# The output weights' product with the gate columns, with the gate columns standing in four column tiles and a summing product behind it

## The chip, the cores and the metric

The kernel runs on one core of a Trainium2 chip. The metric is the device time of one execution in microseconds; the time before is 626.16 us, the median of three runs (625.21 to 626.29).

## What is computed

Sliding-window attention (4 batches, 8 heads, 576 rows, 64 columns a head) is followed by a gated feed-forward layer and a mixture of experts whose choice can be held from row to row. The change lies in the second of the three, where the feed-forward layer's output meets the gate of the third:

```python
h = np.maximum(x @ w_in, 0.0)
# three taps along the rows, then
gate = 1.0 / (1.0 + np.exp(-conv_out))
y = (h * gate @ w_out)                       # (2304, 512)
logits = np.einsum('bsd,de->bse', y, w_gate) # 8 experts
local  = np.einsum('bsd,de->bse', y, w_local) # one more column
...
out[b, s] = p[e] * (np.maximum(y[b, s] @ w1[e], 0.0) @ w2[e])
```

The kernel doesn't form the logits from `y`: it multiplies `w_out` by the nine gate columns once, and appends the ten columns that result (one of them zero) to `w_out`, so that one matmul gives `y` and the logits.

## The kernel before

Rows of the sequence are handled a batch at a time. `ffn(b)` runs over eight blocks of 128 hidden columns (KF = 8) and, for each, two halves of 288 rows: twelve matmuls a half (L470; weights and `x` are held as a high and a low part in fp32r, and three products are summed), then ReLU (L477), three taps and the gate on ACT and DVE (L489 to L493), and a split of the gated block into `gH` and `gL` (L498, L499). `ffn_out(i)` (L512) multiplies 128 rows of the gated block with `woutH` and `woutL`, in two column halves; the second half (260 wide) holds the ten gate columns. `attention(b + 1)` runs beside `ffn(b)`: transposes (L201, L214), scores (L247), softmax (L259 to L284), transposes of the weights (L297, L299) and the product with `v` (L324), whose result is split into `x` by L334 on ACT and L337 on DVE.

The change lies in `conv_out(kk)`, which is called once for each of the eight 128-row blocks of `w_out`, all within `ffn(0)`. The weights come as 64-bit floats: `bits64` (L597, L599, L601, all on DVE) makes a 32-bit block `lf`, and `finish` makes of it

- `woutH` and `woutL` (L629 on ACT, L630 on DVE),
- `psWT`, four transposes on PE (L648), copied by ACT to `wt` (L649),
- `psW`, `wt` times the gate columns `wgl`, four fp32 matmuls that add up in one PSUM bank with `wt` standing and ten columns moving (L652),
- the appended columns of `woutH` and `woutL` (L654 on ACT, L655 on DVE).

`wgl` is filled at the start by two DMAs that POOL issues (L676, L677) behind that of the taps (L675, into `cr`), and its last column is zeroed by DVE (L672). `ident` and `mask` are made on POOL ahead of that.

In this part of the program the order on each engine is set when the kernel is built, by a scheduler that plays the instructions through with the lengths that it assumes; each engine then runs its list in that order. `psWT`, `psW` and the tiles of attention take turns in the four PSUM banks of the pool `psa`; `wt` and the output tiles `ysb` take turns in the two buffers of the pool `y`. The first 54 us or so and the last part (the experts) are written in an order of their own.

Of the kernel before, what the change touches and what calls it, by code (L numbers as in the profile page):

```python
# [8 lines left out]
F32 = mybir.dt.float32  # L9
# [4 lines left out]
AF = mybir.ActivationFunctionType  # L14
# [7 lines left out]
def kernel(  # L22
# [14 lines left out]
    nc = tc.nc  # L37
    w_in, conv_w, w_out = (a.bitcast(U32) for a in (w_in, conv_w, w_out))
    P = 128
    B, H, S, D = q.shape  # L40
    DM = H * D
    FF = w1.shape[2]
    KD = DM // P
    KF = FF // P
    E = w1.shape[0]
# [13 lines left out]
    const = ctx.enter_context(tc.tile_pool(name="const", bufs=1))  # L59
# [8 lines left out]
    ident = const.tile([P, P], F32, name="ident")  # L68
# [5 lines left out]
        nc.gpsimd.affine_select(out=m, in_=m, pattern=[[1, P]], compare_op=ALU.is_ge, fill=NEG, base=-1, channel_multiplier=-1)  # L74
        nc.gpsimd.affine_select(out=m, in_=m, pattern=[[-1, P]], compare_op=ALU.is_ge, fill=NEG, base=64, channel_multiplier=1)
    cw = const.tile([P, 3, KF], F32, name="cw")
    wgl = const.tile([P, KD, E + 2], F32, name="wgl")
    L_all = const.tile([P, NT, E + 2], F32, name="L_all")


    E1 = E + 2
# [4 lines left out]
    psa = p1l.enter_context(tc.tile_pool(name="psa", bufs=4, space=PSUM))  # L86
# [12 lines left out]
    if True:  # L99
# [21 lines left out]
        def bank(b):  # L121

            cyc[0] += 1
            i = cyc[0] % 8
            if b == 0 and i % 4 == 1:
                return psm.tile([P, 512], F32, tag="m", name="psM")
            if b == 0 and i % 4 == 3:
                return pso.tile([P, 512], F32, tag="o", name="psO")
            return psa.tile([P, 512], F32, tag="a", name="psA")
# [47 lines left out]
        def warm(ps, n):  # L177

            w = ident.bitcast(BF16)
            for _ in range(n):  # L180
                nc.tensor.matmul(ps[:, 0:256], w[:, 0:P], w[:, 0:256], start=True, stop=True)
# [411 lines left out]
        def bits64(r, f, steps=range(3)):  # L593

            hi, lo, fb = r[:, :, 1], r[:, :, 0], f.bitcast(U32)
            if 0 in steps:
                nc.vector.tensor_scalar(fb, hi, 3, 0x3FFFFFF8, op0=ALU.logical_shift_left, op1=ALU.bitwise_and)  # L597
            if 1 in steps:
                nc.vector.scalar_tensor_tensor(fb, hi, 0xC0000000, fb, op0=ALU.bitwise_and, op1=ALU.bitwise_or)  # L599
            if 2 in steps:  # L600
                nc.vector.scalar_tensor_tensor(fb, lo, 29, fb, op0=ALU.logical_shift_right, op1=ALU.bitwise_or)  # L601
# [3 lines left out]
        def chunk_in(c, kk):  # L605
            src = w_in.rearrange("(k p) f -> p k f", p=P)
            return src[:, kk, 2 * c * CC:2 * (c + 1) * CC]

        def load_chunk(r, src, eng=nc.sync):
            eng.dma_start(out=r.rearrange("p f t -> p (f t)"), in_=src)  # L610
            return r
# [3 lines left out]
        def quarters(t):  # L615

            return t.rearrange("p (a k i) -> p k a i", k=KD, i=QB)
# [4 lines left out]
        def conv_chunk(src, wH, wL, eng, r=None, view=lambda t: t):  # L622
            if r is None:
                r = load_chunk(cv.tile([P, CC, 2], U32, name="raw", bufs=2), src)
            f = cv.tile([P, CC], F32, name="lf")
            bits64(r, f)

            def finish():
                nc.scalar.activation(wH, view(f), AF.Copy)  # L629
                eng.tensor_tensor(wL, view(f), wH.bitcast(F32), op=ALU.subtract)  # L630

            return f, finish
# [5 lines left out]
        def conv_out(kk):  # L638

            src = w_out.rearrange("(k p) f -> p k f", p=P)  # L640
            f, fin = conv_chunk(src[:, kk, :], quarters(woutH[:, kk, 0:DM]), quarters(woutL[:, kk, 0:DM]), nc.vector, view=by_tile)

            def finish():
                fin()
                wt = y_p.tile([P, KD, P], F32, tag="ysb", name="wt")
                pt = psa.tile([P, 512], F32, tag="a", name="psWT")
                for j in range(KD):
                    nc.tensor.transpose(pt[:, j * P:(j + 1) * P], f[:, j * P:(j + 1) * P], ident)  # L648
                nc.scalar.activation(wt.rearrange("p j f -> p (j f)"), pt, AF.Copy)  # L649
                ps = psa.tile([P, 512], F32, tag="a", name="psW")  # L650
                for j in range(KD):
                    nc.tensor.matmul(ps[:, 0:E1], wt[:, j, :], wgl[:, j, :], start=j == 0, stop=j == KD - 1)  # L652
                wH, wL = woutH[:, kk, DM:DW], woutL[:, kk, DM:DW]
                nc.scalar.activation(wH, ps[:, 0:E1], AF.Copy)  # L654
                nc.vector.tensor_tensor(wL, ps[:, 0:E1], wH.bitcast(F32), op=ALU.subtract)  # L655

            return finish
# [11 lines left out]
        with tc.manual_schedule():  # L669
            warm(bank(0), 6)  # L670
            load_pair(0, 0)
            nc.vector.memset(wgl[:, :, E + 1:E1], 0.0)  # L672
            KC = 3 * KF
            taps = cv.tile([P, CC, 2], U32, tag="raw", name="cr", bufs=2)[0:KC, 0:P]
            nc.gpsimd.dma_start(out=taps.rearrange("r p t -> r (p t)"), in_=conv_w.rearrange("k (f x) -> (k f) x", f=KF))  # L675
            nc.gpsimd.dma_start(out=wgl[:, :, 0:E], in_=w_gate.rearrange("(k p) e -> p k e", p=P))  # L676
            nc.gpsimd.dma_start(out=wgl[:, :, E:E + 1], in_=w_local.rearrange("(k p) e -> p k e", p=P))  # L677
            cin = [(c, kk) for c in range(FF // CC) for kk in range(KD)]
            load_pair(0, 1)

            def stage_chunk(i, eng=nc.sync):
                c, kk = divmod(i, KD)
                early[c, kk] = load_chunk(st_p.tile([P, CC, 2], U32, name=f"raw{i}"), chunk_in(c, kk), eng)

            for i in range(2):
                stage_chunk(i, nc.scalar)
            for i in range(2, KD):
                load_pair(0, i)
                stage_chunk(i)
            part = {}  # L690

            def others(s_, i, g):

                c, kk = divmod(i, KD)
                fs = slice(c * CC, (c + 1) * CC)
                if s_ == "c":
                    if g == 0:
                        part[i] = cv.tile([P, CC], F32, name="lf")
                    bits64(early[c, kk], part[i], (g,))
                elif s_ == "h":  # L700
                    cin.pop(0)
                    nc.scalar.activation(winH[:, kk, fs], part[i], AF.Copy)
                elif s_ == "u":
                    nc.gpsimd.tensor_tensor(winL[:, kk, fs], part[i], winH[:, kk, fs].bitcast(F32), op=ALU.subtract)
                elif s_ == "w":
                    part["f"] = cv.tile([P, CC], F32, tag="lf", name="cf")[0:KC, 0:P]
                    bits64(taps, part["f"])
                elif s_ == "W":
                    part["ps"] = bank(0)
                    nc.tensor.transpose(part["ps"][:, 0:KC], part["f"], ident[0:KC, 0:KC])  # L710
                elif s_ == "Y":
                    nc.vector.tensor_copy(cw.rearrange("p k f -> p (k f)"), part["ps"][:, 0:KC])
                elif s_ == "D":
                    warm(bank(0), i)
                else:
                    nc.gpsimd.memset(qbds[i], 0.0)
                    load_pair(1, i)
                    if i == 0:
                        stage_chunk(4)
                        stage_chunk(5)  # L720

            attention_first(FIRST, others)
# [3 lines left out]
        y_p = p1l.enter_context(tc.tile_pool(name="y", bufs=2))  # L726
# [853 lines left out]
```

## Time and profile before

| | |
|---|---|
| median of three runs | 626.16 us |
| the profiled execution | 626.18 us |
| its span, first to last instruction | 624.5 us |
| mean granted clock of PE | 0.982 |
| PE busy | 593.2 us, 95% |
| DVE busy | 431.0 us, 69% |
| ACT busy | 386.9 us, 62% |
| POOL busy | 221.7 us, 36% |

A share of the whole span is an average over stages that have different limits. The stretch in which the eight blocks of `w_out` are prepared, 59 to 119 us, is a tenth of the span and is best read by itself. Matmuls overlap in the records, and their ends are modelled: the time from one start to the next says more than the length of one. An fp32 matmul stands in the trace as two weight loads and two matmuls, and in an order listing as one row.

### The profile page before, as it was taken

The page shows a single profiled execution, that of the slowest core. Times are in us where ns is not written, and L with a number is a line of the kernel's source. Part 1 is how long each engine was busy: PE and PEld are TensorE (multiplying, and loading weights), DVE is VectorE, ACT ScalarE, POOL GpSimd, SP SyncE. Part 2 cuts the span into 40 slices and gives each one's busy share as a digit, 9 for nine tenths or more (in the row PEclk, how much of TensorE's full clock was granted, in tenths as well). Part 3 has the DMA queues.
Part 4 walks back from the last instruction along what each step waited for, and adds up shares of the span by engine and source line. Part 5 has one row for each costly group of instructions (what it writes and reads, how often), then busy time and mean ns, then how long its engine had stood idle before and what let it go on. Part 6 is the DMA issues. An engine that isn't in the chain of part 4 may idle for free.

```text
span 624.5 us, 12744 instructions
## 1 busy us (share of the span) xinstructions
PE 593.2 (95%) x4503; PEld 533.9 (85%) x4503; DVE 431.0 (69%) x986; ACT 386.9 (62%) x910; POOL 221.7 (36%) x251
## 2 busy tenths in 40 slices
PE   6779999999999999999999989999999999999996
PEld 4658998899999999989987879979899799897774
DVE  4888999645786167852786977658766686576863
ACT  3567778535876357853661556566765676667863
POOL 3412000001223012342250257458567385643740
PEclk9789999799999999999999999999999999999999
DMA  8794515653245201129102289768668763524850
GB/s 188 187 233 120 165 59 114 111 130 82 53 83 100 70 35 37 35 64 273 46 2 34 93 242 358 265 223 292 218 219 307 247 222 123 179 69 144 295 174 16
DMA packets 122614, 92.17 MB, mean 148 GB/s; under 512 B 96594, under 2 KB 97170, under 8 KB 122544
## 3 DMA queue, kind: packets, MB, share of 16 engines
q1 hardware_dynamic: 116064, 79.61, 44.4%
q0 software_dynamic: 4992, 10.24, 4.9%
q10 hardware_dynamic: 1488, 1.44, 0.8%
q8 instruction: 37, 0.61, 0.4%
q14 instruction: 33, 0.27, 0.1%
HBM read 89.53 MB, written 10.71 MB: 161 GB/s over the span
## 4 chain that ended last, share of the span: by engine, by line
PE 61%; DVE 13%; ACT 9%; DMA 9%; issue 5%; SPq 2%; POOL 0%; POOLq 0%; DVEq 0%; ACTq 0%
PE psM L470 14%; PE psO L512 13%; PE psH L1327 8%; PE psO L1362 8%; PE psA L247 3%; PE psO L1341 3%; ACT x L1168 3%; DMA raw<-in_moe_w_dram 3%; PE psA L324 2%; DMA pcur<-p_dram,gidx 2%; PE psA L299 2%; DMA qk<-in_q_dram 2%; DMA raw<-in_moe_w_out_dram 1%; ACT woutH L1168 1%; PE psG L582 1%
## 5 line engine op out<-in xcount | busy, mean ns | idle before, releaser
L499 POOL TENSOR_TENSOR gL<-h,gH 128x64 fp32r<-128x64 f32 (+5 forms) x46 | 43.6, 956 | 216.0 <-ACT gH L498 209.2
L470 PE MATMUL psM<-x,winH 128*128 128x288 f32 x512 | 108.4, 303 | 0.1
L470 PEld LDWEIGHTS psM<-x,winH 128*128 128x128 f32 x512 | 82.0, 189 | 2.4 <-ACT x L334 0.4
L470 PE MATMUL psM<-x,winL 128*128 128x288 f32 x256 | 76.0, 297 | 0.0
L512 PE MATMUL psO<-woutH,gH 128*128 128x262 f32 (+2 forms) x240 | 64.4, 314 | 1.2 <-ACT gH L498 1.0
L512 PE MATMUL psO<-woutL,gH 128*128 128x262 f32 (+2 forms) x240 | 62.2, 305 | 0.0
L512 PE MATMUL psO<-woutH,gL 128*128 128x262 f32 (+2 forms) x240 | 61.2, 304 | 0.0
L1253 POOL DMA_INDIRECT out_dram<-o,sidx x24 | 31.6, 1319 | 79.6 <-ACT o L1295 41.6
L271 ACT ACTIVATE sS<-sS,mx 128x128 f32<-128x128 f32 (+1 forms) x144 | 55.1, 386 | 6.9 <-DVE mx L259 6.8
L1172 DVE TENSOR_TENSOR woutL<-raw,woutH 128x1024 fp32r<-128x1024 f32 x28 | 33.8, 1224 | 29.1 <-ACT woutH L1168 29.1
L1172 DVE TENSOR_TENSOR x<-raw,x 128x1024 fp32r<-128x1024 f32 x42 | 49.9, 1222 | 4.0 <-ACT x L1168 3.8
L1362 PE MATMUL psO<-gH,x 128*128 128x288 f32 x240 | 51.3, 296 | 0.0
L1327 PE MATMUL psH<-gH,woutH 128*128 128x288 f32 x160 | 48.3, 302 | 0.4 <-DVE gL L1330 0.4
L470 PEld LDWEIGHTS psM<-x,winL 128*128 128x128 f32 x256 | 48.4, 189 | 0.1
L1327 PE MATMUL psH<-gL,woutH 128*128 128x288 f32 x160 | 47.4, 296 | 0.0
L1327 PE MATMUL psH<-gH,woutL 128*128 128x288 f32 x160 | 47.3, 295 | 0.0
L512 PEld LDWEIGHTS psO<-woutH,gH 128*128 128x128 f32 x240 | 41.0, 190 | 4.1 <-ACT gH L498 1.6
L1168 ACT ACTIVATE x<-raw 128x1024 fp32r<-128x1024 f32 x42 | 43.0, 1056 | 0.0
L512 PEld LDWEIGHTS psO<-woutL,gH 128*128 128x128 f32 x240 | 41.4, 191 | 1.4
L512 PEld LDWEIGHTS psO<-woutH,gL 128*128 128x128 f32 x240 | 40.9, 191 | 1.2
L259 DVE CUSTOM_DVE_ANT_0 sS<-psA,mask 128x128 f32<-128x128 f32 (+1 forms) x126 | 28.8, 277 | 17.9 <-PE psA L247 15.1
L1362 PEld LDWEIGHTS psO<-gH,x 128*128 128x128 f32 x240 | 39.8, 189 | 0.0
(395 smaller groups left out, 1645.5 us busy)
## 6 DMA issues: line engine op xcount, KB each, us to landing
raw<-in_moe_w_dram SPq DMA_DIRECT2D x104, 512.0 KB
v<-in_v_dram SPq DMA_DIRECT2D x56, 128.0 KB
y_dram<-ysb SPq DMA_DIRECT2D x17, 256.0 KB
raw<-in_moe_w_out_dram SPq DMA_DIRECT2D x8, 512.0 KB
raw<-in_moe_w_dram SPq DMA_DIRECT2D x32, 128.0 KB
raw<-in_moe_w_in_dram SPq DMA_DIRECT2D x6, 512.0 KB
qk<-in_k_dram SPq DMA_DIRECT2D x32, 72.0 KB
qk<-in_q_dram SPq DMA_DIRECT2D x32, 72.0 KB
```

The source lines that it names most:

```text
L247: nc.tensor.matmul(ps[:, j * P + lo:(j + 1) * P], qbd[:, c, :], kT[:, k0:W * (c + 1)], start=True, stop=True)
L259: nc.vector.tensor_tensor_reduce(sS[:, c, lo:P], ps[:, j * P + lo:(j + 1) * P], mask[:, lo:P], -scale, -NEG, op0=ALU.add, op1=ALU.min, acc ...
L271: nc.scalar.activation(sS[:, c, lo:P], sS[:, c, lo:P], AF.Exp, scale=-1.0, bias=mx[:, c:c + 1], accum_out=sume[:, c:c + 1],)
L470: nc.tensor.matmul(ps[:, 0:HS], wt[:, kk, f * P:(f + 1) * P], xt[:, c0:c0 + HS], start=n == 0, stop=n == 3 * KD - 1,)
L499: e1.tensor_tensor(gL[:, f, r:r + m], t[:, done:done + m], gH[:, f, r:r + m].bitcast(F32), op=ALU.subtract)
L512: nc.tensor.matmul(p_[:, 0:cs.stop - cs.start], gt[:, kk, r:r + P], wt[:, kk, cs], start=n == 0, stop=n == 3 * KF - 1,)
L1168: nc.scalar.activation(dst[kk][0], raws[kk], AF.Copy)
L1172: nc.vector.tensor_tensor(L_, raws[kk], H_.bitcast(F32), op=ALU.subtract)
L1253: nc.gpsimd.indirect_dma_start(out=out[:, :], out_offset=bass.IndirectOffsetOnAxis(ap=sidx[0:n, c:c + 1].bitcast(U32), axis=0), in_=o[0:n] ...
L1327: nc.tensor.matmul(ps, a, w, start=n == 0, stop=n == 3 * KD - 1)
L1341: nc.tensor.matmul(ps, a[:, f], w, start=n == 0, stop=n == 3 * KF - 1)
L1362: nc.tensor.matmul(ps, a, w[:, f], start=n == 0, stop=n == 3 * KF - 1)
```

## The change

`wgl` has 32 columns for each of the four blocks of 128 model columns instead of ten; DVE zeroes the 23 behind the gate columns. The four matmuls of `finish` now have `wgl` standing and `wt` moving: each gives 32 rows of 128 columns, in its own quarter of the PSUM partitions (four column tiles), and they don't add up in PSUM. ACT copies the 128x128 result to a new tile `w4`, and a fifth matmul, `psV`, has `w4` standing and a selector `sel` moving, which adds the four quarters and gives the ten columns with the 128 rows on the partitions, as before. `sel` is four pieces of `ident` under one another, made by four POOL copies at the start. `w4` is taken from the pool `y` and `psV` from the pool `psa`.

```diff
-    wgl = const.tile([P, KD, E + 2], F32, name="wgl")
+    wgl = const.tile([P, KD, 32], F32, name="wgl")
+    sel = const.tile([P, E + 2], F32, name="sel")
+    for i in range(0, P, 32):
+        nc.gpsimd.tensor_copy(sel[i:i + 32], ident[i:i + 32, i:i + E + 2])
...
                 for j in range(KD):
-                    nc.tensor.matmul(ps[:, 0:E1], wt[:, j, :], wgl[:, j, :], start=j == 0, stop=j == KD - 1)
+                    nc.tensor.matmul(ps[32 * j:32 * j + 32, 0:P], wgl[:, j, :], wt[:, j, :], start=True, stop=True)
+                w4 = y_p.tile([P, DM], F32, tag="ysb", name="w4")
+                nc.scalar.activation(w4[:, 0:P], ps[:, 0:P], AF.Copy)
+                ps = psa.tile([P, 512], F32, tag="a", name="psV")
+                nc.tensor.matmul(ps[:, 0:E1], w4[:, 0:P], sel, start=True, stop=True)
...
-            nc.vector.memset(wgl[:, :, E + 1:E1], 0.0)
+            nc.vector.memset(wgl[:, :, E + 1:32], 0.0)
```

The scheduler gives the instructions of `ffn(0)` and `attention(1)` another order on PE, ACT and DVE; behind that part the orders are alike but for a few loads. Line numbers of the changed kernel are 3 higher up to the product and 7 higher behind it. Three places at the end of that part follow.

PE before, the last two blocks of `w_out` (`psWT` are the transposes, `psW` the product):

```order
L648 MATMUL psWT<-ident,lf 128x128 [waits DVE_49]
L648 MATMUL psWT<-ident,lf 128x128 x3
L512 MATMUL psO<-woutH,gH 128x262 [waits Activation_49]
L470 MATMUL psM<-x,winH 128x288 [waits Activation_49] x2
L652 MATMUL psW<-wgl,wt 128x10 [waits Activation_49]
L652 MATMUL psW<-wgl,wt 128x10 x3
L512 MATMUL psO<-woutL,gH 128x262 [waits DVE_49]
L512 MATMUL psO<-woutH,gL 128x262
L512 MATMUL psO<-woutH,gH 128x260 [waits Activation_49]
L648 MATMUL psWT<-ident,lf 128x128 [waits DVE_49]
L648 MATMUL psWT<-ident,lf 128x128 x3
L512 MATMUL psO<-woutH,gH 128x262 [waits Activation_49]
```

PE now, from the last `psW` but one on (`psV` is the summing product, `w_` a copy `w4`):

```order
L473 MATMUL psM<-x,winH 128x288 [waits Activation_49]
L473 MATMUL psM<-x,winH 128x288 [waits DVE_49]
L473 MATMUL psM<-x,winL 128x288
L473 MATMUL psM<-x,winH 128x288 [waits DVE_49]
L473 MATMUL psM<-x,winL 128x288
L655 MATMUL psW<-wt,wgl 32x128 [waits Activation_49]
L655 MATMUL psW<-wt,wgl 32x128 x3
L659 MATMUL psV<-sel,w_1558 128x10 [waits Activation_49]
L651 MATMUL psWT<-ident,lf 128x128 [waits DVE_49,PE_49]
L651 MATMUL psWT<-ident,lf 128x128 x3
L515 MATMUL psO<-woutH,gH 128x260 [waits Activation_49]
L515 MATMUL psO<-woutL,gH 128x260 [waits DVE_49]
```

Ahead of the second last `psW` there now stand four matmuls of `ffn(1)`, two of which want DVE's split of `x`; and `psV` stands right behind `psW`. The last row here is followed by the last `psW` and its `psV`.

ACT before, at the same place (`qbd` and `x` belong to attention):

```order
L225 ACTIVATE qbd_127<-psA 64x8x64 [waits PE_49]
L225 ACTIVATE qbd_127<-psA 64x8x64
L498 ACTIVATE gH<-h 128x576 [waits DVE_49]
L629 ACTIVATE woutH<-lf 128x4x4x32 [waits DVE_49]
L334 ACTIVATE x<-psA 128x320 [waits PE_49]
L334 ACTIVATE x<-psA 128x256 [waits PE_49]
L649 ACTIVATE wt<-psWT 128x512 [waits PE_49,Activation_49]
L654 ACTIVATE woutH<-psW 128x10 [waits PE_49]
L629 ACTIVATE woutH<-lf 128x4x4x32 [waits DVE_49]
L649 ACTIVATE wt<-psWT 128x512 [waits PE_49,Activation_49]
L654 ACTIVATE woutH<-psW 128x10 [waits PE_49]
```

ACT now:

```order
L632 ACTIVATE woutH<-lf 128x4x4x32 [waits DVE_49]
L228 ACTIVATE qbd_132<-psA 64x8x64 [waits PE_49]
L228 ACTIVATE qbd_132<-psA 64x8x64
L337 ACTIVATE x<-psA 128x320 [waits PE_49]
L337 ACTIVATE x<-psA 128x256 [waits PE_49]
L652 ACTIVATE wt<-psWT 128x512 [waits PE_49,Activation_49]
L657 ACTIVATE w_1558<-psW 128x128 [waits PE_49,Activation_49]
L661 ACTIVATE woutH<-psV 128x10 [waits PE_49]
L652 ACTIVATE wt<-psWT 128x512 [waits PE_49,Activation_49]
L657 ACTIVATE w_1578<-psW 128x128 [waits PE_49,Activation_49]
L524 ACTIVATE ysb<-psO 128x262 [waits Activation_49]
L661 ACTIVATE woutH<-psV 128x10 [waits PE_49]
```

The last L629 (L632 now) has moved ahead of `qbd`, `x` and the second last `wt`, and the copies `w_` stand between `wt` and the appended columns.

DVE before, from the last block's bits (L601) on:

```order
L601 SCALAR_TENSOR_TENSOR lf<-raw,lf 128x512 [waits DVE_49]
L282 TENSOR_SCALAR sS<-sS,sume 128x64 [waits DVE_49]
L284 TENSOR_TENSOR sS<-sS,sume 128x1024
L337 TENSOR_TENSOR x<-psA,x 128x320 [waits Activation_49]
L337 TENSOR_TENSOR x<-psA,x 128x256 [waits Activation_49]
L655 TENSOR_TENSOR woutL<-psW,woutH 128x10 [waits Activation_49]
L630 TENSOR_TENSOR woutL<-lf,woutH 128x4x4x32 [waits Activation_49]
L655 TENSOR_TENSOR woutL<-psW,woutH 128x10 [waits Activation_49]
```

DVE now:

```order
L604 SCALAR_TENSOR_TENSOR lf<-raw,lf 128x512 [waits DVE_49]
L285 TENSOR_SCALAR sS<-sS,sume 128x64 [waits DVE_49]
L287 TENSOR_TENSOR sS<-sS,sume 128x1024
L221 COPY kT_134<-psA 128x512 [waits PE_49]
L633 TENSOR_TENSOR woutL<-lf,woutH 128x4x4x32 [waits Activation_49]
L340 TENSOR_TENSOR x<-psA,x 128x320 [waits Activation_49]
L340 TENSOR_TENSOR x<-psA,x 128x256 [waits Activation_49]
L207 COPY kT_134<-psA 128x64 [waits PE_49]
L211 COPY qbd_132<-psA 64x64
L212 COPY qbd_132<-psA 64x64
L662 TENSOR_TENSOR woutL<-psV,woutH 128x10 [waits Activation_49] x2
```

The last L601 (L604 now) has the `kT` and `qbd` copies behind it that stood ahead of it. In the whole list up to the last L655 DVE has the same operations as before; ACT has the eight copies more and one output copy (L521) that stood later; and by its last product PE has run eight matmuls more, two each of L470 with `winH` and with `winL`, and two each of L512 with `woutL` and with `gL`.

## Rows read from the trace of the kernel before

**Rows 1.** The page, part 1: busy us, share of the span and instructions of each engine

```profile
PE 593.2 (95%) x4503; PEld 533.9 (85%) x4503; DVE 431.0 (69%) x986; ACT 386.9 (62%) x910; POOL 221.7 (36%) x251
```

**Rows 2.** Busy time by stretches of 10 us, 59 to 119 us: last stretch and sum

```profile
core 0: us, PE busy (x) PEld busy (x) DVE busy (x) ACT busy (x) POOL busy (x), PEclk, DMA share, GB/s
...
109.00:119.00 10.00, 9.11 (x88) 7.79 (x88) 9.36 (x23) 5.60 (x14) 0.00 (x0) 0.94 0.71 128
sum 60.00, PE 56.51 PEld 52.87 DVE 58.51 ACT 46.06 POOL 0.00; mean PE 9.42 PEld 8.81 DVE 9.75 ACT 7.68 POOL 0.00
```

**Rows 3.** The same view, one stretch behind the stage

```profile
135.00:175.00 40.00, 40.00 (x362) 38.63 (x362) 25.36 (x83) 26.39 (x92) 5.61 (x8) 1.00 0.39 81
```

**Rows 4.** Groups by line, 60 to 119 us: busy us, mean ns, idle before, releasers

```profile
L652 PE MATMUL psW<-wgl,wt 128*128 128x10 f32 x64 | 8.4, 260 | 2.0 <-ACT wt L649 1.9
L652 PEld LDWEIGHTS psW<-wgl,wt 128*128 128x128 f32 x64 | 8.1, 197 | 3.0 <-ACT wt L649 3.0
```

**Rows 5.** Timeline of the PE weight loads: start us, us, engine, line, tiles

```profile
64.59 0.99 PEld L652 LDWEIGHTS psW<-wgl,wt 128*128 128x128 f32 x8
65.50 0.75 PEld L247 LDWEIGHTS psA<-kT,qbd 128*128 128x128 f32 x6
66.17 0.47 PEld L214 LDWEIGHTS psA<-ident,qk 128*128 128x128 f32 x4
...
92.99 0.66 PEld L324 LDWEIGHTS psA<-aT,v 128*64 128x64 f32 x20 [0.17 <-issue]
93.72 0.19 PEld L470 LDWEIGHTS psM<-x,winL 128*128 128x128 f32 x1
```

**Rows 6.** Timeline of the end of the stage: ACT, DVE, PE, PE weight loads

```profile
110.56 1.20 ACT L225 ACTIVATE qbd<-psA 64x512 f32<-64x512 f32 x2 [0.74 <-PE psA L214]
...
113.01 0.71 ACT L334 ACTIVATE x<-psA 128x320 fp32r<-128x320 f32 x2
...
115.36 0.18 ACT L654 ACTIVATE woutH<-psW 128x10 fp32r<-128x10 f32 x1 [1.15 <-PE psW L652]
115.53 0.63 ACT L629 ACTIVATE woutH<-lf 128x512 fp32r<-128x512 f32 x1
116.52 0.60 ACT L649 ACTIVATE wt<-psWT 128x512 f32<-128x512 f32 x1 [0.35 <-PE psWT L648]
...
113.60 0.21 DVE L204 COPY kT<-psA 128x64 f32<-128x64 f32 x1
...
114.82 0.68 DVE L601 SCALAR_TENSOR_TENSOR lf<-raw,lf 128x512 uint32<-128x512 uint32 x1
115.42 0.25 DVE L282 TENSOR_SCALAR sS<-sS,sume 128x64 f32<-128x64 f32 x1
115.58 1.22 DVE L284 TENSOR_TENSOR sS<-sS,sume 128x1024 f32<-128x1024 f32 x1
116.83 0.82 DVE L337 TENSOR_TENSOR x<-psA,x 128x320 fp32r<-128x320 f32 x2
...
117.64 0.68 DVE L630 TENSOR_TENSOR woutL<-lf,woutH 128x512 fp32r<-128x512 f32 x1
...
114.27 1.06 PE L652 MATMUL psW<-wgl,wt 128*128 128x10 f32 x8
...
117.17 1.32 PE L652 MATMUL psW<-wgl,wt 128*128 128x10 f32 x8 [0.56 <-ACT wt L649]
...
118.27 1.40 PEld L247 LDWEIGHTS psA<-kT,qbd 128*128 128x128 f32 x6
```

**Rows 7.** Busy time by stretches: the stretch at the lower granted clock

```profile
118.00:124.00 6.00, 6.00 (x29) 5.93 (x29) 1.87 (x14) 2.60 (x13) 0.00 (x0) 0.50 0.63 96
```

**Rows 8.** Timeline of the start: POOL issues the taps, DVE uses them

```profile
2.95 0.75 POOL L675 DMA_DIRECT2D cr<-in_moe_conv_w_dram  x1
...
11.04 0.20 DVE L597 TENSOR_SCALAR cf<-cr 24x128 uint32<-24x128 uint32 x1
...
13.40 0.69 DVE L218 COPY kT<-psA 128x512 f32<-128x512 f32 x1 [0.45 <-PE psA L214]
```

## The prediction

> **What bounds the kernel now.** I read the page's shares first. PE is busy 95% of the span and DVE 69% [rows 1], so one would price the change by what it takes off PE. The change touches only the eight finishes of `conv_out`, though, and they all lie between 59 and 119 us; so I next read the busy time by stretches of that stage. There DVE is busy 58.5 of 60 us, and the PE's 56.5 holds modelled ends and waits [rows 2]. The reader is to see that this stage ends when DVE is through its list: DVE also takes apart the 64-bit weights (L597 to L601), and PE fills in with what is ready. Behind the stage it is the reverse: from 135 to 175 us PE is busy 40.00 of 40 us and DVE 25 [rows 3], and much the same beyond. So whatever delays the moment at which PE is free of the last product is passed on to the end, and what PE does ahead of that moment is taken off again. The groups by line show the product itself: 64 passes on PE, eight for each finish, with 2.0 and 3.0 us of waiting for the ACT copy `wt` before them, in 4 and 5 places [rows 4].
>
> **The product on PE.** Each fp32 matmul is two passes of weight load and matmul. Eight passes with 128 columns standing and 10 moving take from 64.59 to 65.50 us, 0.91 [rows 5], and 8 x 0.91 = 7.3 us in all. Now 32 columns stand and 128 move. No row has four column tiles. From above: L247 has 128 standing and 128 moving, six passes from 65.50 to 66.17, 0.11 each, which is 0.89 for eight: nothing saved. From below: L324 runs 64-column tiles in two halves, 20 passes of 64 moving columns from 92.99 to 93.72, 0.037 each [rows 5]; doubled for 128 columns that is 0.58 for eight, and half of it with four tiles instead of two, 0.29. I take 0.45, between the two readings of L324, the nearest row. The sum behind it is one matmul of the old kind, two passes, 0.91/4 = 0.23. Ahead of L324 the load queue stood 0.17 us for nothing but issue [rows 5]; I charge it once a product. So 0.45 + 0.23 + 0.17 = 0.85 for 0.91: PE saves 8 x 0.06 = 0.5 us, with bounds from 0.29 + 0.23 (3.1 us saved) to 0.89 + 0.23 + 0.17 (3.0 lost).
>
> What L324 shows is that two column halves do overlap, and that entering them costs about 0.17 us. The Trainium skill (TensorEngine Tiling (Array Packing), Performance Considerations) recommends this very swap of standing and moving operand with column tiling, with up to four times the throughput where the free side is 32 or less; its Key Properties say that a change of tiling mode drains TensorE. By the first rule alone the product would cost 0.91/4 = 0.23 and PE would save 3.6 us, an estimate from that page; the second speaks against it, and the 0.17 us agrees with it.
>
> **ACT and the new hop.** Each finish gains a copy of 128x128 out of PSUM. ACT takes 0.18 us for 128x10 and 0.60 for 128x512 [rows 6], so about 0.28; 8 x 0.28 = 2.2 us on an engine that is busy 46 of 60 us in the stage [rows 2]: hidden but for the end. The wait is what counts: the summing matmul `psV` waits for the copy, PE is in order, and in four finishes `psV` stands right behind `psW` with nothing between. Three of them are the last three.
>
> **The end of the stage, walked through.** Up to its last product the DVE list holds the same operations in both kernels, so DVE's share would again be done near 117.64 + 0.68 = 118.3 us [rows 6]. Before, the last block's bits (L601) end at about 115.4, and behind them come 1.4 us of softmax, two `x`, and the rest [rows 6]. Now `x`, the `kT` and `qbd` copies and L630 all stand behind the last L601: 0.16 + 1.25 + 0.6 (kT) + 0.6 (L630) + 0.8 (x) + 0.6 (three small copies) = 4.0 us, so it ends at 114.3. ACT then has L629 0.63, two `qbd` 1.20, two `x` 0.71 ahead of the second last `wt` [rows 6]: 114.3 + 0.63 + 1.2 + 0.7 + 0.6 = 117.4. On PE the second last `psW` stands behind four matmuls of the next batch which want that `x` from DVE: 114.3 + 0.16 + 1.25 + 0.6 + 0.6 + 0.8 = 117.7, and two matmuls, 118.0. From there two finishes run one after the other, PE and ACT in turn. Rows give the hops: product to ACT is the passes and 0.18 (114.27 to 115.36, less 0.91); `wt` to product is 0.65 (116.52 to 117.17) [rows 6]. So `psW` 118.0, copy 118.6, `psV` 118.95, the last transposes 119.2, `wt` 119.2 + 0.45 + 0.18 = 119.85, `psW` 120.5, copy 121.1, `psV` 121.45, and PE is free at 121.7. Before it was free at 118.27 [rows 6]. That is +3.4 us. The earlier finishes cost the end nothing while DVE stays full: what hides them is DVE's list, and if DVE were not full they would cost up to 0.4 us each where `psV` stands behind `psW`.
>
> **What is done ahead.** By its last product the changed kernel has executed four matmuls of L470 and four of L512 more than before. At 362 matmuls in 40 us [rows 3], 8 x 0.11 = 0.9 us comes off again.
>
> **The start.** Four small POOL copies build `sel` ahead of the three weight DMAs, and one mask operation moves ahead of them too. The tap load `cr` is issued at 2.95 us now, and DVE wants it at 11.04; a landing some 0.9 us later (estimate: four copies like the small POOL memsets and a mask operation) might hold DVE for a few tenths, but DVE stands idle 0.45 us at 13.40 behind that anyway [rows 8]. Taken at 0, with +0.5 as the bound. The wider memset of `wgl` runs on an idle DVE. SP's loads are only reordered among themselves; 0.
>
> **The sum.** The profiled execution took 626.18 us (span 624.5), beside a median of 626.16, so no correction: 626.2 + 3.4 - 0.9 = **628.7 us**, +0.4%. A measurement of this kernel can tell about 0.2%, 1.25 us, from no change.
>
> **The clock** is the largest unknown. Behind the thinly filled end of the stage the granted clock is 0.50, that is 1.2 GHz, from 118 to 124 us with PE busy all of the time [rows 7]; those 6 us do 3 us of work. I leave it as it is, since PE again waits often just before; without that stretch the time would be 3 us lower, and with one twice as long 3 us higher.
>
> **Rivals.** (a) *PE's saving counts in full, and the tail does not grow:* it needs PE and not DVE to end the stage. For it speak PE's 95%; against it DVE's 58.5 of 60. With four tiles at the lower bound, 3.1 us saved: 623.1; with 0.45 and no switching charge, 8 x 0.23 = 1.8 saved: 624.4. It decides if DVE shows idle time in the stage that it did not have. (b) *The clock stays full at 119 to 125:* 628.7 - 3 = 625.7, within 0.2%. For it: the gaps are spread differently; against: they are longer. (c) *The new hop is hidden,* because the last `L601` comes early and something else ends the stage: the tail costs 1 us instead of 3.4, 626.3. (d) *The column tiles do not overlap:* 0.89 for 0.45, twice in the tail, +0.9: 629.6. (e) *The clock falls earlier and stays low for twice as long:* 631.7.
>
> **How the numbers follow.** Forecast 0.44; (d) 0.05; (e) 0.08: slower together 0.57. (b) 0.12 and (c) 0.10: same 0.22. (a) 0.14, and 0.07 for (b) and (c) together, 623.3: faster 0.21. The range takes in the forecast, (b), (c), (d) and most of (e), and part of (a): 624.2 to 631.7.
>
> **What would show it.** Right: DVE still above 9.5 of 10 us up to 117; the last product off PE at 121 to 122.5 instead of 118.3; the last two `psV` with waits of about 0.4 us for ACT; the stretch from 135 on as before. The product's eight passes at 0.3 to 0.6 us. Wrong: DVE with new idle time in the stage (the walk then starts from a false time), the low-clock stretch gone or doubled, or a last `psV` at or before 119.

## The result

The changed kernel takes 633.12 us (median of 4 runs, 631.39 to 633.85), the kernel before 625.68 beside it (623.65 to 626.29): a ratio of 1.0117, 95% interval 1.0091 to 1.0143. It is 7.4 us slower where 2.5 were forecast, and outside the range. Measured once more, it was 633.46 for 626.19 us, 1.0136 (1.0104 to 1.0168). The profiled execution took 633.46 us with a span of 631.7, 7.2 over the span of before.

For the kernels e1 to g3 and i1 to i3 I read the trace up to the first gather of the experts (at 362 to 377 us) and give no time, since beside them the kernel before, too, took 661 to 677 us (medians) and their expert weights came in more slowly from about 380 us on (158 to 178 GB/s from 480 to 520 us, 246 in before); the kernels h1 to h4 have times.

**The profile after.** Lines behind the product have other numbers than before (L470 is L473, L601 L604, L630 L633, L655 L662). The page's shares, for [rows 1], tell nothing:

```profile
PE 593.3 (94%) x4519; PEld 530.0 (84%) x4519; DVE 432.0 (68%) x986; ACT 389.7 (62%) x918; POOL 223.1 (35%) x255
```

Busy time by stretches (PE, PE loads, DVE, ACT, POOL, granted clock, DMA share, GB/s), for [rows 2], [rows 3] and [rows 7]:

```profile
core 0: us, PE busy (x) PEld busy (x) DVE busy (x) ACT busy (x) POOL busy (x), PEclk, DMA share, GB/s
...
109.00:119.00 10.00, 7.50 (x66) 6.39 (x67) 8.70 (x29) 6.16 (x22) 0.00 (x0) 0.83 0.37 84
119.00:129.00 10.00, 8.76 (x96) 7.47 (x93) 5.37 (x23) 6.20 (x19) 0.00 (x0) 1.00 0.86 151
...
112.00:115.00 3.00, 3.00 (x17) 3.00 (x15) 1.80 (x10) 1.77 (x5) 0.00 (x0) 0.50 0.08 29
...
139.00:175.00 36.00, 36.00 (x334) 34.87 (x332) 21.42 (x68) 23.01 (x77) 5.00 (x6) 1.00 0.41 83
```

DVE is no longer full up to the end of the stage (8.70 of 10 us from 109 to 119, 9.36 in before), the 1.2 GHz stretch now lies in the stage (112 to 115 us) and not behind it, and behind the stage PE is full as before. The groups of the product, 60 to 127 us, for [rows 4]:

```profile
L655 PE MATMUL psW<-wt,wgl 128*32 128x128 f32 x64 | 3.4, 285 | 2.0 <-ACT wt L652 2.0
L659 PE MATMUL psV<-sel,w 128*128 128x10 f32 x16 | 2.8, 248 | 2.5 <-ACT w L657 2.5
L657 ACT ACTIVATE w<-psW 128x128 f32<-128x128 f32 x8 | 2.2, 272 | 2.5 <-PE psW L655 2.4
L655 PEld LDWEIGHTS psW<-wt,wgl 128*32 128x32 f32 x64 | 1.3, 108 | 3.5 <-ACT wt L652 2.8 <-issue 0.7
```

The tiled product is cheap, 3.4 us in all for 8.4; the sum takes 2.8, and PE stands 2.5 us before it for the copy `w4` (named `w` here).

**Where the 7.2 us lie.** Four marks cut the execution: DVE's restart on a `raw` load near 60 us (all lists up to there are the same, `sel` copies aside), the last `woutL` from the product (end of the stage), the first transpose of the gate (`psG<-ident,lgs`), and the first gather of a unit on POOL. DVE's rows with a wait, before and then after (time, duration, wait and releaser in brackets):

```profile
58.59 0.43 DVE L597 TENSOR_SCALAR lf<-raw 128x512 uint32<-128x512 uint32 x1 [1.00 <-DMA raw<-in_moe_w_in_dram]
...
118.74 0.17 DVE L655 TENSOR_TENSOR woutL<-psW,woutH 128x10 fp32r<-128x10 f32 x1 [0.41 <-ACT woutH L654]
```

```profile
61.35 0.43 DVE L600 TENSOR_SCALAR lf<-raw 128x512 uint32<-128x512 uint32 x1 [1.16 <-DMA raw<-in_moe_w_in_dram]
...
95.11 0.43 DVE L600 TENSOR_SCALAR lf<-raw 128x512 uint32<-128x512 uint32 x1 [0.81 <-PE psWT L651]
113.60 0.29 DVE L262 CUSTOM_DVE_ANT_0 sS<-psA,mask 128x128 f32<-128x128 f32 x1 [1.20 <-PE psA L250]
124.27 0.17 DVE L662 TENSOR_TENSOR woutL<-psV,woutH 128x10 fp32r<-128x10 f32 x1 [1.52 <-ACT woutH L661]
126.78 0.17 DVE L662 TENSOR_TENSOR woutL<-psV,woutH 128x10 fp32r<-128x10 f32 x1 [2.34 <-ACT woutH L661]
```

In the second pair, h1 and h2 are the two kernels executed once more.

| us, changed less before | first pair of executions | second pair (h2, h1) |
|---|---|---|
| up to DVE's restart | +2.76 (61.35, 58.59) | -0.83 (58.52, 59.35) |
| the stage, restart to last `woutL` | +5.28 (65.43, 60.15) | +6.95 (66.81, 59.86) |
| from there to `psG` | -3.65 (209.17, 212.82) | -0.71 (210.79, 211.50) |
| `psG` to the first gather | +3.09 (35.88, 32.79) | +2.97 (35.80, 32.83) |
| gather to the end | -0.28 (259.87, 260.15) | -1.38 (258.88, 260.26) |
| span | +7.20 | +7.00 |

Two terms are in both pairs: a stage that is 5 to 7 us longer, and 3 us between `psG` and the gather. The 3.65 us of the first pair fit the 0.9 us done ahead and some 3 us for the 1.2 GHz stretch of [rows 7], which stood behind the stage in before; in the second pair both kernels have such a stretch from 119 to 129 us (mean clock 0.83 in each), and 0.71 is left, near to the 0.9.

### The profile page after: what moved, and what is told of

Read it like the earlier page. It is cut to its first block, busy times and chain, and to the rows that moved or that the text cites. A ratio compares the mean times of both kernels' runs of the same rounds, so it can differ in the third digit from the quotient of the medians.

```text
span 631.7 us, 12799 instructions
## 1 busy us (share of the span) xinstructions
PE 593.3 (94%) x4519; PEld 530.0 (84%) x4519; DVE 432.0 (68%) x986; ACT 389.7 (62%) x918; POOL 223.1 (35%) x255
## 4 chain that ended last, share of the span: by engine, by line
PE 62%; DVE 17%; DMA 8%; ACT 7%; issue 5%; POOL 0%; ACTq 0%; POOLq 0%; DVEq 0%
PE psM L473 13%; PE psO L515 13%; PE psH L1334 9%; PE psO L1369 8%; PE psO L1348 4%; PE psA L250 3%; ACT x L1175 3%; PE psA L327 2%; DMA pcur<-p_dram,gidx 2%; PE psA L302 2%; DMA raw<-in_moe_w_in_dram 2%; PE psH L1316 2%; DVE sS L262 1%; DVE lf L602 1%; DVE lf L604 1%
## 5 line engine op out<-in xcount | busy, mean ns | idle before, releaser
L473 PE MATMUL psM<-x,winH 128*128 128x288 f32 x512 | 108.4, 302 | 1.9 <-DVE x L340 1.6
L473 PEld LDWEIGHTS psM<-x,winH 128*128 128x128 f32 x512 | 81.6, 188 | 5.1 <-DVE x L340 2.1
L473 PE MATMUL psM<-x,winL 128*128 128x288 f32 x256 | 75.4, 294 | 0.0
L515 PE MATMUL psO<-woutL,gH 128*128 128x262 f32 (+2 forms) x240 | 63.7, 305 | 0.5 <-DVE woutL L633 0.5
L473 PEld LDWEIGHTS psM<-x,winL 128*128 128x128 f32 x256 | 48.1, 188 | 0.0
```

The source lines that it names most:

```text
L473: nc.tensor.matmul(ps[:, 0:HS], wt[:, kk, f * P:(f + 1) * P], xt[:, c0:c0 + HS], start=n == 0, stop=n == 3 * KD - 1,)
L515: nc.tensor.matmul(p_[:, 0:cs.stop - cs.start], gt[:, kk, r:r + P], wt[:, kk, cs], start=n == 0, stop=n == 3 * KF - 1,)
```

## The experiments

In each the stage runs from DVE's restart to the last `woutL`. It is cut once more at the start of DVE's last bits (L601 of before), since they release the last finish. The last column is the time in the stage at a granted clock of 0.50, that is 1.2 GHz. The *hop* is the copy `w4` on ACT and the sum `psV` behind it.

| kernel | restart to last bits | last bits to last `woutL` | stage | of it at 1.2 GHz |
|---|---|---|---|---|
| before, two executions | 56.23, 56.21 | 3.92, 3.65 | 60.15, 59.86 | 0.9, 0.3 |
| changed, two | 56.97, 57.42 | 8.46, 9.39 | 65.43, 66.81 | 3.4, 7.1 |
| e1 `sel` copies alone | 56.36 | 3.84 | 60.20 | 0.8 |
| e2 changed, `sel` copies late | 56.04 | 9.15 | 65.19 | 3.4 |
| g1, h3 changed, store on ACT | 57.03, 56.65 | 8.45, 8.45 | 65.48, 65.10 | 3.4, 3.5 |
| e6 first six finishes new | 56.79 | 7.83 | 64.62 | 3.5 |
| e7, f4, i1 last two new | 55.98, 56.26, 56.41 | 3.79, 3.79, 3.79 | 59.77, 60.05, 60.20 | 0, 0, 0 |
| i3 last two new, store on ACT | 56.19 | 3.80 | 59.99 | 0 |
| f1 hop, no tiles | 59.44 | 11.58 | 71.02 | 15.0 |
| f2 tiles, no hop | 56.78 | 2.86 | 59.64 | 0 |
| f3, g3, i2 sum deferred | 57.07, 58.56, 57.16 | 3.76, 3.77, 3.76 | 60.83, 62.33, 60.92 | 0, 3.4, 0 |
| g2 only the fifth new | 55.52 | 7.50 | 63.02 | 3.4 |
| h4 only the first new | 58.14 | 4.70 | 62.84 | 3.0 |

**The start.** Theory: the later restart is the execution's. Rival: the `sel` copies on POOL hold up the loads behind them. e1 adds only the copies to the kernel before:

```
+    sel = const.tile([P, E + 2], F32, name="sel")
+    for i in range(0, P, 32):
+        nc.gpsimd.tensor_copy(sel[i:i + 32], ident[i:i + 32, i:i + E + 2])
```

> The kernel before with only the four small POOL copies that build sel, which nothing reads; every other engine has its list of before. If these copies, by holding the tap and gate loads on POOL's queue, make the 1.4 us by which the first L470 came later (57.16 for 55.79 us), the time is 1.0 to 1.5 us over before. If the start only took another course of the clock in that execution, it is within 0.5 us of before, and its first L470 falls anywhere from 55.5 to 57.5. I expect the second.

e2 moves them behind the three weight loads of the changed kernel.

> The changed kernel with the four sel copies behind the three weight loads on POOL; every other engine has its list of the changed kernel. If the copies ahead of the loads cost the start, the time is 1.0 to 1.5 us under the changed kernel, about 631.8 beside a before of 625.7; if not, it is within 0.7 us of it, 632.4 to 633.8. I expect the second.

e1 restarts at 61.05 us (first L470 at 56.42), e2 at 60.49. But e7 below, with the copies ahead of the loads, restarts at 58.39, and h1 and h2, which are the two kernels once more, at 59.35 and 58.52: the changed kernel is now the earlier one; and f1 below, which has no `sel` at all, restarts at 61.10. With the same lists the 18 executions of experiments lie between 58.39 and 61.53. The 2.76 us of the first pair are chance.

> The kernel before, unchanged, for another profiled execution. The stage (DVE's restart on the raw load to the last woutL) took 60.15 us in its first and should take 60 to 60.3 again; the restart stood at 58.59 us, where the other kernels, with the same lists up to there, had 58.39 to 61.49. If the first 58 us vary between executions, the restart is now somewhere from 58.4 to 61.5; if the early restart is the kernel's own, it is at 58.4 to 58.8 again.

> The changed kernel, unchanged, for another profiled execution and time. Stage 65.2 to 65.6 us (65.43, and 65.19 and 65.48 in the two kernels with the same lists there), gather 35.6 to 36 us behind the psG transposes. If the start varies between executions, DVE's restart is anywhere from 58.4 to 61.5 us; if the late one is its own, 61 to 61.6.

In h2 the stage is 66.81 us and not 65.2 to 65.6; its clock is 0.71 from 109 to 119 us, for 0.83 in the first execution, and 7.1 us of the stage lie at 1.2 GHz, for 3.4.

**Which finishes.** e6 has the new product in the first six finishes and the old one in the last two, e7 the other way:

```
+                if kk < KF - 2:          (e7: kk >= KF - 2)
                     ...four column tiles, w4, psV
+                else:
+                    for j in range(KD):
+                        nc.tensor.matmul(ps[:, 0:E1], wt[:, j, :], wgl[:, j, 0:E1], start=j == 0, stop=j == KD - 1)
```

> The first six finishes have the column tiles, the copy and the sum; the last two have the old product. The prediction's account, by which earlier finishes cost the end nothing and only the last two hops count, gives before + 0 to 0.7, 625.7 to 626.5. The theory now, that the earlier hops empty DVE's list in the stage (3.3 us of new idle time, and perhaps 1.4 from the start), gives before + 3.5 to 5.5, 629 to 631.

> The last two finishes have the column tiles, the copy and the sum; the first six have the old product. The prediction's account (the whole loss lies in the tail) gives the changed kernel's time or near it, before + 2.5 and more. The theory now gives the two hops alone, before + 1.0 to 2.5, 626.7 to 628.2, with the end of the stage 1 to 2.5 us later than 118.27 and the idle time of DVE from 59 to 109 us as before (about 0.8 us in all).

Neither account held for e7: its two hops cost nothing, 59.77 us for 60.15, though they are the last two. PE has other matmuls between its `psW` and `psV`, and no wait before `psV` shows. e6, where the last two finishes are those of before, has nearly the whole loss, 64.62, and 7.83 us behind the last bits, for 8.46 with the new product in all eight. So the loss at the end of the stage comes from earlier finishes; the last two hops' own share is some 0.6 us.

**Hop or tiles.** f1 keeps the old product and adds a copy and a second matmul; f2 has the tiles, without copy and sum:

```
f1, behind the old product:
+                w4 = y_p.tile([P, DM], F32, tag="ysb", name="w4")
+                nc.scalar.activation(w4[:, 0:E1], ps[:, 0:E1], AF.Copy)
+                ps = psa.tile([P, 512], F32, tag="a", name="psV")
+                nc.tensor.matmul(ps[:, 0:E1], ident, w4[:, 0:E1], start=True, stop=True)
f2, in the changed kernel: the four lines of w4 and psV are left out
```

> The product of before, on all eight finishes, with a copy of its 10 columns out of PSUM and a second matmul against ident behind it: the hop without column tiles; its order of instructions is near that of the changed kernel. The stage is measured from DVE's restart on a raw load (58.59 us in before, 61.35 in the changed kernel) to the last woutL on DVE: 60.15 us in before and 65.43 in the changed kernel. If the hop makes the loss, the stage is 64.5 to 67 us, and the time is before + 5 to 8 us. If the column tiles make it (entering and leaving their mode), the stage is 60 to 62 us.

> The product in four column tiles, with neither copy nor sum: the gate columns of woutH and woutL are read from the tiled product as it stands, so that part of the computation is left out, tokens go to other experts, and only the trace up to 330 us and the stage can be compared. If the hop makes the loss, the stage is 59 to 60.5 us (60.15 in before, 65.43 in the changed kernel); if the column tiles make it, 63 to 66.

The hop it is: 71.02 us with it and the old product, 59.64 with the tiles alone. f1 is over its range, in part by its clock (0.66 from 99 to 109, 0.83 up to 129): 15 us at half the clock can make up to 7.5 of its 10.9 us. The tiles cost the stage nothing; the 0.2 to 0.5 us by which it is shorter are no more than lies between executions of one kernel (0.4 in e7).

**The hop's wait, or the order that follows from it.** The scheduler (the planner of the expectations) sets the order by lengths that it assumes, and a hop moves every later choice. f3 leaves all eight hops in, but puts each sum behind the transposes of the next finish:

```
+                if totals:
+                    totals.pop(0)()          (psV, woutH, woutL of the finish before)
                 nc.scalar.activation(wt.rearrange("p j f -> p (j f)"), pt, AF.Copy)
```

> The changed kernel with the sum of each finish, and its gate columns, moved behind the transposes of the next finish; the last one stands alone behind the loop. The copy and the sum are all there, but PE does not wait for the copy, save at the last. If PE standing before psV makes the loss, the stage falls to 60.5 to 62 us and the time to before + 0 to 2 us. If the added work or the column tiles make it, the stage stays at 64 to 66 us.

The stage is 60.83 us, and 60.92 and 62.33 in two more executions (the last with a clock of 0.83 from 69 to 79). Tiles, copies and sums are all there, so their work is not what costs. g3's other 1.4 us are the clock and 0.5 us more in which DVE waits for loads. The last finishes on PE, with `psV` of one finish in front of the wait for the next `wt`:

```profile
117.83 0.65 PE L653 MATMUL psWT<-ident,lf 128*128 128x128 f32 x4
118.32 0.29 PE L665 MATMUL psV<-sel,w 128*128 128x10 f32 x2
119.23 0.43 PE L659 MATMUL psW<-wt,wgl 128*32 128x128 f32 x8 [0.34 <-ACT wt L656]
120.32 0.29 PE L665 MATMUL psV<-sel,w 128*128 128x10 f32 x2
```

g2 has one hop only, in the fifth finish (`kk == 4` in the condition above), far from the end:

> Only the fifth finish has the tiles, the copy and the sum; the other seven have the old product. One hop can cost PE and DVE at most about 1 us of waiting. But the planner's order is another already: behind the last bits of DVE's list stand x, kT, qbd and L630, near to the changed kernel. Stage from DVE's restart on the raw load to the last woutL: 60.15 us in before, 65.43 in the changed kernel. If the order that the planner makes of a hop is the cause, the stage is 62 to 65.5 us; if each hop's own wait is, 60 to 61.

With one hop, and 0.9 us of PE's wait at `psV`, the stage is 2.9 us longer, and the end of it looks like the changed kernel's, with the old product in the last two finishes. DVE and PE of g2:

```profile
115.16 0.68 DVE L604 SCALAR_TENSOR_TENSOR lf<-raw,lf 128x512 uint32<-128x512 uint32 x1
...
118.16 0.69 DVE L633 TENSOR_TENSOR woutL<-lf,woutH 128x512 fp32r<-128x512 f32 x1
118.89 0.42 DVE L340 TENSOR_TENSOR x<-psA,x 128x256 fp32r<-128x256 f32 x1
...
122.66 0.17 DVE L666 TENSOR_TENSOR woutL<-psW,woutH 128x10 fp32r<-128x10 f32 x1 [2.27 <-ACT woutH L665]
...
111.88 1.06 PE L663 MATMUL psW<-wgl,wt 128*128 128x10 f32 x8 [1.24 <-ACT wt L652]
...
118.92 1.06 PE L663 MATMUL psW<-wgl,wt 128*128 128x10 f32 x8 [0.36 <-ACT wt L652]
119.83 0.63 PE L651 MATMUL psWT<-ident,lf 128*128 128x128 f32 x4
...
121.45 0.96 PE L663 MATMUL psW<-wgl,wt 128*128 128x10 f32 x8
```

The last bits even start earlier than in before (55.52 us behind the restart for 56.2). But both last finishes now stand behind them, one after the other: the second last `psW` is at 118.92, 3.8 us behind the bits, and the last at 121.45. In before the second last `psW` started at 114.27, ahead of the bits [rows 6], and only one finish is left behind them. The third last `psW`, at 111.88, is 52.24 us behind the restart; in before it is 49.95:

```profile
108.54 1.06 PE L652 MATMUL psW<-wgl,wt 128*128 128x10 f32 x8 [0.40 <-ACT wt L649]
```

So 2.3 us are lost before g2's clock falls.

h4 has the one hop in the first finish (`kk == 0`), with the softmax, `kT` and `x` ahead of the last bits:

> Only the first finish has the tiles, the copy and the sum. One hop as in the run with only the fifth, which lost 2.9 us of stage, but here the planner puts x, kT and the softmax of the next batch ahead of the last bits, and the last store stands behind 9 loads. If the order that comes out decides, the stage is 59 to 61 us; if a hop costs some 3 us by itself, 62.5 to 64.

I expected a good stage of that order, and it is 62.84 us: in the range that I had given the rival, a price of 3 us for each hop. The rows tell another reason. Nothing waits before this hop's `psV`. The bits that release the last finish now stand behind the softmax, 1.9 us later in the stage than in before, with nothing left behind them to cover the chain, and the last `psW` meets the low clock (1.71 us for 1.06). The 1.9 us lie ahead of that stretch. The rows:

```profile
115.47 1.22 DVE L287 TENSOR_TENSOR sS<-sS,sume 128x1024 f32<-128x1024 f32 x1
116.61 0.69 DVE L604 SCALAR_TENSOR_TENSOR lf<-raw,lf 128x512 uint32<-128x512 uint32 x1
...
121.31 0.17 DVE L666 TENSOR_TENSOR woutL<-psW,woutH 128x10 fp32r<-128x10 f32 x1 [2.62 <-ACT woutH L665]
...
117.44 0.63 PE L651 MATMUL psWT<-ident,lf 128*128 128x128 f32 x4 [0.85 <-DVE lf L604]
...
119.34 1.71 PE L663 MATMUL psW<-wgl,wt 128*128 128x10 f32 x8
```

Its time is 627.92 us, ratio 1.0036 (1.0021 to 1.0052). A fixed price of 3 us a hop also falls by e7 (two hops, none) and f3 (eight, 0.8 to 2.3). No run here has the changed kernel's order without its hops, so that order decides rests on these four kernels together.

**The clock is a rival, and it was not tested.** Every stage over 62 us has 3 us or more at 1.2 GHz in it, and no stage under 61 us has more than 0.9. g2 and f3:

```profile
113.50:116.50 3.00, 3.00 (x29) 2.31 (x28) 3.00 (x9) 2.02 (x4) 0.00 (x0) 0.50 0.78 126
...
60.00:121.00 61.00, 55.76 (x507) 49.68 (x506) 58.86 (x148) 46.84 (x133) 0.00 (x0) 1.00 0.47 113
```

The first line is g2's, the second f3's; the clock stands ahead of the last two numbers. What a stretch costs is seen where one kernel was executed more than once: g3 is 1.4 to 1.5 us longer than f3 and i2, which have the same lists and no such stretch (0.5 of it are the waits for loads), and h2, with 7.1 us of it, is 1.4 us longer than the first execution, with 3.4. At half the clock 3.4 us can cost 1.7 us at most (an estimate from the two levels). That leaves at least 3.6 of the changed kernel's 5.3 us and 1.2 each of g2's and h4's for waits and order. In the changed kernel all that stands behind the last bits, 8.46 us for 3.92, is at the full clock. Why the clock falls in these stages and not in the others was not shown.

**The store on SP's queue.** Between `psG` and the gather the changed kernel loses 3 us that the stage doesn't explain. SP's issues of before, then of after, with the gather on POOL (L563 is L560 of before, the store of the last half tile to `y_dram`, which the gather reads):

```profile
355.48 5.46 SPq L1149 DMA_DIRECT2D raw<-in_moe_w_dram  x9
361.05 0.36 SPq L560 DMA_DIRECT2D y_dram<-ysb  x1
...
364.35 1.99 POOL L1211 DMA_INDIRECT gH<-y_dram,gidx  x1 [8.86 <-PE psH L1309]
```

```profile
359.90 7.63 SPq L1156 DMA_DIRECT2D raw<-in_moe_w_dram  x12
367.63 0.36 SPq L563 DMA_DIRECT2D y_dram<-ysb  x1
...
371.83 1.00 POOL L1218 DMA_INDIRECT gH<-y_dram,gidx  x1 [11.93 <-DMA raw<-in_moe_w_dram]
...
PE psX L1277 <- DMA gL<-y_dram,gidx: 3.4, 1, 3.4
```

The store stands behind 12 weight loads instead of 9, three issues of 0.6 us each: it is issued 31.7 us behind `psG` for 29.5. The gather follows 4.2 us later for 3.3, and PE waits 3.4 us for what is gathered. The view names a weight load as what released the gather; that it is the store's place shows only in the next two runs. g1 and h3 issue that store on ACT's queue; all other lists are the changed kernel's:

```
-                q_ = nc.sync if half else nc.scalar
+                q_ = nc.scalar
```

> The changed kernel with the last y_dram store (the second half of the last tile) issued on ACT's queue instead of SP's; every other list is that of the changed kernel. On SP it stood behind 12 loads of w1 in the changed kernel and behind 9 in before, and the gather of the first unit, which reads y_dram, was issued 35.8 us behind the gate's transposes (psG) in the changed kernel and 32.8 us behind them in before. If the store's place makes this, the gather now comes 32 to 33.5 us behind the psG transposes and the time is 2 to 3 us under the changed kernel; if the raw weights or PE set it, it stays at 35 to 36.5.

> The changed kernel with the last y_dram store on ACT's queue, for its time. The gather came 32.2 us behind psG for 35.8 in the changed kernel; if PE's wait at the first gathered unit (3.4 us) is the 2.8 us that the changed kernel lost behind psG, the time is 2 to 3.5 us under the changed kernel of this call; if other waits take its place, within 1 us of it.

The gather comes 32.18 and 32.25 us behind `psG`, for 35.88 and 35.80. In h3, which ran beside h2:

```profile
367.92 1.42 POOL L1218 DMA_INDIRECT gH<-y_dram,gidx  x1 [8.31 <-DMA y_dram<-ysb]
```

The time is 629.83 us for 633.46, 3.6 under the changed kernel; against before 1.0064 (1.0040 to 1.0089). So half of the loss is the store's place, and half the stage.

**Versions that might beat both.** f4 and i1 repeat e7, g3 and i2 repeat f3, and i3 is e7 with the store on ACT.

> The first six finishes with the old product and the last two with the tiles, copy and sum, once more. In its first run the stage took 59.77 us and the clock did not fall behind it, and PE came to the transposes of the gate at 327.7 us for 331.6 in before. If that is its own, the time is 2 to 4 us under before; if it was the luck of one execution, within 1 us of before.

> The kernel with the deferred sum once more, for its time. By its first trace it came to the psG transposes 269.95 us behind DVE's restart, for 273.0 in before and 274.65 in the changed kernel, and its gather is not late. If that holds to the end, the time is 2 to 4 us under before (621.5 to 624); if the start and the clock take it back, within 1 us of it.

> The first six finishes with the old product, the last two with tiles, copy and sum, for its time. In two traces its stage was 59.77 and 60.05 us (60.15 and 59.86 in before) and PE came to the psG transposes 269.3 and 269.5 us behind DVE's restart (273.0 and 271.35 in before), with the gather 34.6 and 35.0 us behind psG (32.8 in before). If only the stage's order made the changed kernel slow, the time is 0 to 2 us under before, 624.2 to 626.2; if the tiles, the copy and the sum cost something by themselves, it is over before.

> All eight finishes with the tiles, the copy and the sum, the sum behind the transposes of the next finish, for its time. Stage 60.83 and 62.33 us in two traces, psG 269.95 and 271.5 us behind the restart, gather 32.9 and 32.5 us behind psG. If the order and the exposed chain made the loss, the time is within 2 us of before (624.5 to 628); if the added work did, 630 and more.

> The kernel with the last two finishes new, and the last y_dram store on ACT's queue, where it stands behind no load. If the gather then comes 32 to 33 us behind psG instead of 35, the time is 1 to 2.5 us under that kernel and 1 to 4 us under before; if PE sets the gather there (psX), no change.

All of them are among the kernels without a time, so this stays open. Up to the gather, counted from the restart, before takes 305.8 and 304.2 us, the changed kernel 310.5 and 313.4, e7 and its repeats 303.9 to 304.5, f3 and its repeats 302.6 to 304.1, and i3 302.0. That is level with before or up to some 3 us ahead; whether it lasts to the end was not shown. In i3 the gather comes 32.5 us behind `psG`, for 34.6 to 35.0 in e7 and its repeats.

## Why the prediction was wrong

Two terms of the prediction failed: that DVE's share of the stage would "again be done near" the same time, where 1.9 us of new idle time came, and "SP's loads are only reordered among themselves; 0", where the order cost 3 us. With the walk's 3.4 and the 0.9 done ahead these give 7.4 us, as measured.

**The product on PE: right.** Eight tiled passes show 0.43 us (0.45 taken; 0.36 from the first start to the next matmul in f3's rows, 119.23 to 119.59) and the entry 0.16 (0.17); the sum's loads take 0.24 from start to start (0.23). The Trainium skill (TensorEngine Tiling (Array Packing), Performance Considerations) recommends the swap, with up to four times the throughput; the tiled passes agree in part, at about twice the speed (0.43 us for 0.91), and the whole product is still no cheaper for this stage.

**ACT and the hop: right in size.** The copy takes 0.27 us in the mean (0.28), and the last two `psV` wait 0.46 us each (0.4 expected). The Trainium skill (TensorEngine Tiling (Array Packing), PSUM Bottleneck) says that tiling speeds up TensorE, but not getting the result out of PSUM; the trace agrees: the product saves PE 5.0 us (8.4 to 3.4), and the copy behind it makes PE wait 2.5 and the sum takes 2.8.

**The chain at the end: right.** I walked 7.15 us from the end of the last bits to the last `psV` (114.3 to 121.45). The rows, for [rows 6]:

```profile
118.32 0.68 DVE L604 SCALAR_TENSOR_TENSOR lf<-raw,lf 128x512 uint32<-128x512 uint32 x1
...
121.42 0.81 DVE L340 TENSOR_TENSOR x<-psA,x 128x320 fp32r<-128x320 f32 x2
...
122.74 0.43 PE L655 MATMUL psW<-wt,wgl 128*32 128x128 f32 x8
123.30 0.28 ACT L657 ACTIVATE w<-psW 128x128 f32<-128x128 f32 x1 [0.99 <-PE psW L655]
123.63 0.39 PE L659 MATMUL psV<-sel,w 128*128 128x10 f32 x2 [0.46 <-ACT w L657]
...
125.26 0.43 PE L655 MATMUL psW<-wt,wgl 128*32 128x128 f32 x8 [0.26 <-ACT wt L652]
125.81 0.28 ACT L657 ACTIVATE w<-psW 128x128 f32<-128x128 f32 x1 [0.61 <-PE psW L655]
126.14 0.39 PE L659 MATMUL psV<-sel,w 128*128 128x10 f32 x2 [0.46 <-ACT w L657]
```

The bits end by 118.98, so the last `psV` is 7.16 us behind them.

**"DVE stays full" failed, by 1.9 us.** The walk let the bits end at 114.3, 55.7 us behind the restart at 58.59. They end at 57.6 (61.35 to 118.98). The difference is DVE's new idle time: 0.81 us for 0.19 at the transposes of a finish (95.11), 1.20 at `psA` (113.60), where PE runs at 1.2 GHz, and 0.1 at a load. The first of them is 0.81 or 0.82 in all five executions of this order; the second is 0.37 to 1.63, and 0.37 in e2, whose clock falls only later, at 116.6 us. So some 0.8 of the 1.9 us hang on where the clock fell. DVE's 9.19 of 10 us from 89 to 99 (9.91 in before) was already under the 9.5 that the prediction asked for. I had named this condition and priced it at up to 0.4 us a hop, and I gave the forecast's range nothing for it. The stage's 5.3 us are the walk's 3.4 and these 1.9.

**The store was left out: 3 us.** I compared the order at the end of the stage, took SP's loads at 0 without a row for it, and the stretch behind the stage "as before". SP's list had changed as well, 240 us later, at the one place where a store that is waited for shares the queue with weight loads. It is the largest single miss, and the order could have told it.

**The start was rightly taken at 0,** as the second pair and f1 show, though the tap load is issued 1.2 us later (4.13 for 2.95) and not 0.9; in the first pair chance added 2.76 us.

**The clock: left alone, and it moved.** The stretch behind the stage went in the first pair (rival (b), some 3 us back) and stayed in the second. It took some 2.8 us off the loss in the first pair, and the late start added 2.8; that the first pair's 7.20 us come so near to the sum above is luck in that respect.

**The rivals.** (a) asked for new idle time of DVE as the sign of a faster kernel; it came and meant the opposite, since the chain behind DVE's last bits, and not PE's work, ended the stage. (b) came in the first pair and not in the second. (c) and (d) did not come about. (e) came in part: the clock fell earlier, for 3.4 us in the first execution, and for three such stretches in h2 (108.0, 114.8 and 125.0 us).

## What to carry to other kernels

Where a scheduler orders the work, the price of an edit is not the edit's own work: with one hop of 0.9 us the order behind it changed and the stage was some 3 us longer, up to half of it by the clock. Compare the lists of all engines and queues to the end of the program, and look for the instruction that releases a serial chain (here the last bits, and a store that a gather waits for): what has moved ahead of it, and what has moved behind it. Look at the granted clock in the same stretch before the order is blamed for a difference. Before a faster product is built, ask whether its engine ends the stage at all.

## What was not expected of the hardware

With the same lists, DVE's restart near 60 us lay between 58.39 and 61.53 us over the executions, and the stretch at 1.2 GHz fell in the stage, behind it or in both, so that one pair of traces can be off by 3 us in a single term while the spans agree within 0.2 (7.20 and 7.00).
